# A fused attention and feed-forward kernel: its list of steps in another order, with other buffers and engines for some of them

## The chip, the cores and the metric

One core of one Trainium2 chip runs the whole kernel. The metric is device time in microseconds (us). The core has five engines with queues of their own: TensorE (PE in the profile, with PEld for its weight loads), VectorE (DVE), ScalarE (ACT), GpSimd (POOL), and SyncE (SP), which issues the DMAs. PSUM takes the matmuls' results, SBUF holds the tiles.

## The reference

For 4 batches, 4 heads, 1088 positions and a head dimension of 32, an attention without softmax: queries and keys are sketched with two 8 x 32 matrices, the two sketches are multiplied to 64 features, and the attention is linear in them. Its result, as 4352 tokens of width 128, goes through a multiplicative feed-forward network.

```python
def phi(x):
    a = einsum('rd,bhsd->bhsr', S1, x)
    b = einsum('rd,bhsd->bhsr', S2, x)
    return einsum('bhsi,bhsj->bhsij', a, b).reshape(..., 64)
kv  = einsum('bhsf,bhsd->bhfd', phi(k), v);  z = sum(phi(k), axis=2)
num = einsum('bhsf,bhfd->bhsd', phi(q), kv)
den = einsum('bhsf,bhf->bhs', phi(q), z)[..., None] + 1e-06
x   = (num / den).transpose(0, 2, 1, 3).reshape(4352, 128)
out = (((x @ w1) * (x @ w2)) @ w3) @ w_out        # w1, w2: 128x1024, w3: 1024x1024, w_out: 1024x128
```

## The kernel before

The work is cut into 1181 named steps, each a small function that issues a few instructions. A name has a part ahead of the dot and an action behind it. `ORDER`, a string with all names, is walked once; each step issues its instructions, and every instruction is chained behind the one before it on its engine, so `ORDER` is the order of each engine's queue:

```python
for name in ORDER.split():
    n = len(traced)
    steps.pop(name)()
    ...
for ins, ahead in zip(bulk[UNDER_WAY:], bulk):          # UNDER_WAY = 4
    tc.add_manual_dep(ins, ahead.name, landed, reason="under way")
```

The second loop lets a bulk load go out only when the fourth bulk load ahead of it has landed. Tiles come from pools with a fixed number of buffers ("b" 8, "l" 13, "m" 32, "s" 8, "x" 3, "raw" 3, "q_m" 2); the strings in `SLOTS` say which buffer each tile takes, in the order of allocation, and a tile waits until the readers of that buffer's last tile are done. `POOL` lists the steps on GpSimd instead of VectorE, `CPV` the copies from PSUM on VectorE instead of ScalarE. `WARM` gives idle matmuls that only keep TensorE running, one step `warm{i}` for each entry. The strings were printed by a planner that isn't in the kernel.

The parts, as they follow each other in the main:

- `k0` to `k3`, `kr0`, `kr1`: a batch's keys and values. `lead`, `rest` (line 651) and `gram` (659) build the keys' Gram sums, `T` and `N` (883 to 912) small products, `G` and `ab` (745) sketches, `kp` (677) their products of 128x1024, `kv` (769) their sum with v, `kq` the form that the queries need.
- `q0` to `q4`, `q6`, `qr`: queries. `A`, `C`, `st`, `sh`, `sl`, `sc` (1365 to 1421) make sketches, `al`, `p01`, `p12`, `p2`, `dn`, `de`, `rc`, `bs`, `na` to `nn` (1426 to 1490) denominators and scaled sketches, `phi` (1509) their products, `pT` (1517) transposes them on VectorE, `x` (1527) is 128 matmuls of 32x32 tiles that give the attention's result, `xT` (1540) copies it out of PSUM. `ns` (1494, 1497) is one multiplication and 16 small copies on GpSimd.
- `w1` to `w10`: blocks of weights; `load`, then `c` (263), `m` (484), `j` (495), `a` (501), which turn the float64 words into float32. `f0` to `f7` multiply w3 and w_out into one matrix w3o: `t` (528) transposes a block, `m` (534) multiplies, `o` (538) copies it out. `v.`, `o.S` and the `s` steps of h4 and h6 form sums of blocks.
- `g0` to `g3`: the feed-forward network on 512 tokens each. For each eighth of the hidden width, `a` (1799) and `b` (1809) are two full matmuls each, `c` (1804) copies a to SBUF, `m` (1815) multiplies it by b on VectorE, `o` (1835) are two matmuls with w3o. `oT` (1842), `oS` (1848) and `st` (1556) send the result out.
- `h4`, `h6`: the same for 1024 tokens each with the products saved by a scheme of seven: products `a`, `b` (1673) of half the rows, two of which share the array; copies `ac` to `bi` (1680, 1685); `m11` to `m22` (1707, 1712) and sums `T1` to `T4` (1727 to 1742); products `P1` to `P7` (1759); sums `k1` to `k9` (1767 to 1785).
- `gr`: the network on the 256 remaining tokens.

Of the kernel before, what the change touches and what calls it, by code (L numbers as in the profile page):

```python
# [53 lines left out]
    g4.oS g5.oS g6.oS g7.oS h4.0T2 h4.0T3 h4.0T4 h4.0m11 h4.0m12 h4.0m22 h4.1T1 h4.1T3 h4.1m11  # L54
    h4.1m12 h4.2m11 h4.2m12 h4.2m22 h4.3T4 h4.s2 h6.0T1 h6.0T2 h6.0T4 h6.0m12 h6.0m22 h6.1T1 h6.1T2
    h6.1m11 h6.1m12 h6.1m22 h6.2T4 h6.2m11 h6.2m12 h6.s1 h6.s2 h6.s4 k0.Nf k0.Nh k0.Nr k0.kp1 k1.Nr
    k1.kp1 k2.Nr k2.kp0 k2.kp1 k2.rest0 k3.Nr k3.kp0 k3.kp1 q0.al q0.p01 q0.phi1 q0.sca q1.al q1.p01
    q1.p12 q1.phi q1.sca q2.bs q2.phi0 q3.al q3.bs q3.p01 q3.p12 q3.p2 q3.phi0 q3.sc q3.sl q4.nn
    q4.p2 q4.phi0 q4.phi1 q4.sc q6.al q6.p12 q6.phi1 q6.sc q6.sl qr.p01 qr.p12 s.KS s.Pp s.blk
    s.blkh s.low s.rest  # L60
# [25 lines left out]
w0.load k1.lead0 q0.xc0 q0.xc1 k0.kq w1.a1 k2.max q0.xt1 k1.ab q0.xT0 q0.xT1 g0.4a q1.load g0.5a q1.sm q1.Ct q1.st  # L86
q1.sh k1.rest0 w0.m1 g0.4b g0.6a q1.sl q1.scy q1.sca g0.7a q1.p01 q1.al k1.abt k1.gram0 k1.gram1 k1.gram2 k1.gram3
k1.gram4 q1.p2 w0.c1 w0.c0 g0.4c w0.j1 q3.tr g0.7b g0.5b kr1.abc q3.max q1.p12 k1.Gm q1.dn k1.Gt k1.Ga k1.Gb q1.de
w9.load kh2.load q1.rc q1.bs w0.j0 g0.4m w0.a1 k1.Gc g0.5c g0.7c g0.7m k1.T0 k1.T1 g0.2a v1.zero q1.phi q3.l2 s.AR
# [5 lines left out]
q3.sh k2.T0 k1.kv2 k1.kv3 k1.kv1 k2.T1 k1.kvr k1.kvc kr1.kp g1.2c k2.Ta q2.p12 q2.dn q2.de k2.Tb g0.0m q2.rc g0.6m
q3.sl q3.sc q3.p01 w9.j g1.7m q1.restT q2.bs g1.6a g1.6c w2.c v2.zero q2.phi0 g1.2b k3.loadr g1.3a g1.3c g1.0a g1.5b
g1.3b k1.kqt warm12 w6.c w6.m g0.3b k1.kq g1.5c g1.4a k3.max g1.4c w5.load g1.1b v2.loadr kh3.load k0.Nr q2.load g1.3m
g1.5m g1.2m g1.0c q2.pT0 warm13 g1.0b k2.Tc q2.x g0.3m w9.a1 w5.m q2.xT0 k3.kT0 k2.N0 k2.N1 w5.c q3.al q3.p2 q3.p12
q3.dn w6.j g1.0m q3.de w7.load w2.m g1.4b w7.m w7.c w3.load w10.load w4.load v2.load w2.j k2.Na g1.4m k2.Nb q3.rc
k3.kT1 k3.lead0 q2.restT q3.bs g0.2b g2.6a g2.3a g2.1a g2.5a g2.4a g2.2a w5.j g1.1m g0.2m q3.phi0 k2.Nr g2.2b g2.0a  # L100
g2.3c g2.2c g2.4b g2.5c w3.c g1.6b k3.rest0 w9.a0 g2.4c w2.a0 g2.1c w2.a1 q4.tr k3.gram0 w6.a0 w5.a1 f6.t g2.2m
k3.gram1 k3.gram2 k3.gram3 k3.gram4 q3.pT0 f6.m g2.6b g2.6c g2.0c k3.Gm v.t g2.1b k3.Gt k3.Ga k3.Gb w7.j g2.4m q4.max
g2.7a g2.3b g1.6m q4.l2 w3.m k3.Gc w7.a0 g2.0b f6.o g2.3m w5.a0 w6.a1 v3.zero g2.1m q3.x q4.l1 k3.T0 k3.T1 g2.6m w3.j
g2.7c q4.rm g2.5b g2.5m q3.xT0 q3.load g2.7b g3.0a v3.load w8.load v3.loadr k3.Ta w4.m g3.0c g3.0b g3.0m g3.3a g3.1b
g3.1a g3.3c k3.Tb w3.a0 g3.1c g2.0m k2.kp1 q6.tr k3.Tc g2.7m w7.a1 f4.t g3.6a q3.restT g3.6c q4.A0 w3.a1 q6.max k3.ab
k3.N0 k3.abt k2.kp0 q4.C0 q4.C1 k3.N1 f4.m k3.kp1 g3.6b f0.t f3.t f4.o k3.kp0 f0.m q4.At q6.l2 g3.6m k2.kv0 k2.kv3
g3.1m w4.c w4.j k3.kv0 k3.kv1 k3.kv3 k3.kv2 k3.kvr q4.Ct q4.sm q6.l1 qr.max k3.kvc k2.kv1 k2.kv2 k2.kvr k2.kvc f3.m
w8.c f0.o f3.o w4.a1 w4.a0 g3.7a g3.7c g3.4b g2.0o k3.Na q4.st f1.t qr.l2 q6.rm q4.sh w10.m qr.l1 q4.sl q4.sc g3.5a
g3.4a g3.3b f1.m f1.o w10.c g3.4c g3.4m qr.rm k3.Nb q4.p01 w8.m q4.al k3.Nr k3.kqt g2.4o q6.A0 q6.C0 f2.t g3.3m q4.p2
v.3 q6.C1 k3.kq q6.At w8.j w8.a1 q6.Ct g2.6o g3.0o g3.4o qr.A0 qr.C0 qr.C1 qr.Ct q6.sm w10.j q6.st q6.sh q4.p12 w8.a0  # L110
g3.5b q6.sl w10.a1 q6.sc q4.dn qr.At g3.5c q4.de f5.t q4.rc g1.0o g1.1o q4.na q4.bs q4.nb f2.m q4.nm q4.nr qr.sm q6.al
q6.p01 q6.p2 g0.0o g0.1o q6.p12 f2.o g0.2o g0.6o k2.kqt g0.3o q4.ne g3.5m q4.nn q6.dn k2.kq f5.m f5.o g3.7b g3.2b
g1.6o g0.5o g0.4o w10.a0 qr.st f7.t f7.m g3.2a q4.phi0 q4.phi1 qr.sh qr.sl qr.sc f7.o q4.pT0 g3.2c q4.pT1 g2.5o g0.7o
# [1 line left out]
q6.nn v.1 q4.xT1 q6.phi0 q6.phi1 g1.4o o.S3 q4.xT3 g1.2o q6.pT0 g3.5o g3.7m q6.pT1 g1.3o q6.x qr.p2 q6.xT2 qr.p12
qr.dn qr.de g3.1o g1.7o g3.6o g2.1o qr.rc qr.bs q6.xT3 g1.5o q6.xT0 h4.s1 h4.s3 q6.xT1 q6.ns g3.7o g3.2o qr.phi0
qr.pT0 g1.oT qr.x h4.0b5 h4.0a1 qr.xT0 h4.1a1 g2.oT g2.st h4.0b2 g3.oT h4.0a5 h4.0b1 h4.0bd h4.1b1 h4.0ac h4.s2 h4.s4
h4.1ac v.2 h4.0a6 h4.0bc h4.0bh h4.0ae o.S1 h6.s1 h4.0a2 h4.0ah h4.0b3 h4.1b2 o.S2 o.S4 h4.0ad h4.1a6 h6.s2 h4.0a7
h4.0m11 h4.0b6 h4.1a5 g3.st h4.1bc h4.1b6 h4.1ae h4.1bh v.4 h4.0ag h4.0be h4.0bf h4.1b5 h4.0a3 h4.0af h4.0b7 h4.1a7
h4.1be h4.1b7 h4.1ad h4.0a4 h4.0m12 h4.1a2 h4.0bg h4.1bd h4.1b3 h4.1a3 h4.0m22 h4.0b4 h4.1ag h4.2b1 h4.0ai h4.2a1  # L120
h4.1bf h4.2bc h4.2b2 h4.1ah h4.1a4 h4.2a2 h4.2ac h4.1bg h4.1af h4.1m12 h4.1m22 h4.1b4 h4.3b1 h4.2a6 h4.1ai h4.0m21
g1.st h4.2b5 h4.2ae h4.3a1 h4.2bh h4.1m11 h4.2ah h4.1m21 h4.3bc h4.1T1 h4.2m11 h4.3ac h4.2b6 h4.2be h4.2bd h4.0T1
h4.2a5 h4.2ad h4.3a2 h4.3b2 h4.3bh h4.3b6 h4.2a7 h4.2b7 h4.0T3 h4.3a6 h4.3ae h4.2ag h4.2b3 h4.3ah h4.3be h4.2a3 h4.3a5
h4.3ad h4.3b5 h4.3bd h4.2bg h4.2a4 h4.3b7 h4.3a7 h4.1T3 h4.2af h6.1b1 h4.2bf h4.3m11 h4.3a3 h4.2m22 h4.3bg h4.2b4
h4.2ai h4.3ag h4.2m12 h4.3b3 h6.0a1 h4.2m21 h6.0ac h4.3af h4.3a4 h4.1T2 h6.1bc h4.3b4 h6.1a1 h6.0b1 h6.0a6 h4.3ai
h4.3m21 h6.1b6 h4.3bf h4.2T1 h6.1ac h4.0P7 h4.2P1 h4.1P7 h4.0T2 h4.0P1 h4.0T4 h4.1P2 h4.3T1 h4.3m22 h4.1P5 h4.0P4
h6.0bc h4.2P2 h4.0P2 h4.3P5 h4.3m12 h4.2P5 h4.1P6 h4.2T2 h4.2P6 h4.0P5 h4.2T3 h4.1P1 h4.3T3 h4.3P7 h4.2P7 h4.3P1
h4.3T2 h4.3T4 h4.3P6 h4.2T4 h4.2P4 h6.0ae h4.0P6 h4.3P4 h4.1T4 h6.s3 h4.1P4 h4.k1 h4.k3 h4.3P2 h4.k2 h4.0P3 h4.3P3
h4.2P3 h4.k4 h4.k7 h4.1P3 h6.1be h4.k5 gr.1a h6.0b6 gr.1c h6.0be h6.0a7 h6.0b5 h6.0a5 h6.1a6 h6.0ad h6.1b7 h4.k8 h6.s4
# [1805 lines left out]
```

## Time and profile before

| | |
|---|---|
| median of 3 runs | 248.95 us (248.9 to 249.46) |
| the profiled execution | 248.89 us, its span 246.9 us |
| mean granted clock of TensorE | 1.00 |
| busy: PE, DVE, POOL, ACT | 238.4, 212.2, 154.4, 121.8 us |
| instructions | 6753 |
| DMA | 22.06 MB, mean 89 GB/s |

A group's row gives busy time and mean nanoseconds of one, and behind the second bar the engine's idle time ahead of them with what ended it. A row of the timeline gives start and length in us, engine, line, operation and tiles, and in brackets idle time. A row of the chain gives start, length, engine, tile and line. A row of the waits gives who waits for whom, idle time, count and the longest.

### The profile page before, as it was taken

The page shows a single profiled execution, that of the slowest core. Times are in us where ns is not written, and L with a number is a line of the kernel's source. Part 1 is how long each engine was busy: PE and PEld are TensorE (multiplying, and loading weights), DVE is VectorE, ACT ScalarE, POOL GpSimd, SP SyncE. Part 2 cuts the span into 40 slices and gives each one's busy share as a digit, 9 for nine tenths or more (in the row PEclk, how much of TensorE's full clock was granted, in tenths as well). Part 3 has the DMA queues.
Part 4 walks back from the last instruction along what each step waited for, and adds up shares of the span by engine and source line. Part 5 has one row for each costly group of instructions (what it writes and reads, how often), then busy time and mean ns, then how long its engine had stood idle before and what let it go on. Part 6 is the DMA issues. An engine that isn't in the chain of part 4 may idle for free.

```text
span 246.9 us, 6753 instructions
## 1 busy us (share of the span) xinstructions
PE 238.4 (97%) x2726; PEld 133.7 (54%) x2726; DVE 212.2 (86%) x426; ACT 121.8 (49%) x246; POOL 154.4 (63%) x198
## 2 busy tenths in 40 slices
...
GB/s 202 267 167 324 173 204 185 92 229 135 244 177 230 183 230 142 3 4 0 3 0 0 3 1 3 54 73 4 0 0 0 3 11 74 1 0 3 0 53 96
DMA packets 31934, 22.06 MB, mean 89 GB/s; under 512 B 21280, under 2 KB 26528, under 8 KB 31904
## 3 DMA queue, kind: packets, MB, share of 16 engines
...
q8 instruction: 21, 0.34, 0.6%
q14 instruction: 9, 0.07, 0.1%
...
## 4 chain that ended last, share of the span: by engine, by line
PE 80%; DVE 15%; issue 2%; POOL 1%; ACT 0%; DVEq 0%
PE ps_X L1673 11%; PE ps_o L1759 10%; PE a_ps L1799 9%; PE b_ps L1809 9%; PE ps_o L1835 9%; PE ps_w3o L534 6%; PE ps_Y L1673 6%; PE idle_ps L255 4%; PE ps_Z L1673 3%; DVE ab L1815 3%; PE ps_g L659 2%; PE ps_ac L1374 2%; PE ps_kv L769 2%; PE ps_or L1824 2%; DVE pT L1517 1%
## 5 line engine op out<-in xcount | busy, mean ns | idle before, releaser
L1809 PE MATMUL b_ps<-xT,w 128*128 128x512 f32 (+1 forms) x80 | 36.4, 560 | 0.3 <-DVE ab L1815 0.2
L1673 PE MATMUL ps_X<-xd,wv 64*128 64x512 f32 x112 | 35.6, 595 | 0.0
L1799 PE MATMUL a_ps<-xT,w 128*128 128x512 f32 (+1 forms) x80 | 35.4, 558 | 0.0
L1804 ACT COPY ffa<-a_ps 128x512 f32<-128x512 f32 (+1 forms) x34 | 17.6, 536 | 30.4 <-PE a_ps L1799 30.3
L1680 ACT COPY hc<-ps_X 128x512 f32<-128x512 f32 x37 | 20.7, 589 | 21.2 <-PE ps_X L1673 12.9
L1835 PE MATMUL ps_o<-ab,w3o 128*128 128x512 f32 x64 | 29.4, 597 | 0.0
L1815 DVE TENSOR_TENSOR ab<-ffa,b_ps 128x512 f32<-128x512 f32 (+1 forms) x40 | 23.9, 619 | 3.2 <-PE b_ps L1809 2.5
L501 POOL TENSOR_TENSOR w3c<-w3c,cv_m 128x512 int32<-128x512 int32 x16 | 21.0, 1328 | 6.3 <-DVE w3c L495 6.3
L1799 PEld LDWEIGHTS a_ps<-xT,w 128*128 128x128 f32 x80 | 14.4, 190 | 14.6 <-issue 8.5
L1707 POOL TENSOR_TENSOR hc<-hc 128x512 f32<-128x512 f32 x15 | 19.7, 1327 | 2.9 <-DVE hc L1685 2.9
L1673 PEld LDWEIGHTS ps_X<-xd,wv 64*128 64x128 f32 x112 | 15.2, 186 | 10.4 <-issue 8.3
L1809 PEld LDWEIGHTS b_ps<-xT,w 128*128 128x128 f32 x80 | 14.0, 190 | 12.2 <-issue 7.7
L1673 PE MATMUL ps_Y<-xd,wv 64*128 64x512 f32 x48 | 19.2, 599 | 0.0
L1835 PEld LDWEIGHTS ps_o<-ab,w3o 128*128 128x128 f32 x64 | 11.7, 190 | 13.7 <-issue 13.2
L534 PEld LDWEIGHTS ps_w3o<-wo,w3T 128*128 128x128 f32 x128 | 15.3, 192 | 3.2 <-issue 2.5
L534 PE MATMUL ps_w3o<-wo,w3T 128*128 128x128 f32 x128 | 15.9, 277 | 0.6 <-DVE w3T L528 0.6
L1540 ACT COPY xd<-ps_x 64x256 f32<-64x256 f32 x32 | 11.7, 367 | 7.6 <-PE ps_x L1527 7.2
L538 ACT COPY w3o<-ps_w3o 128x128 f32<-128x128 f32 x8 | 2.0, 270 | 26.3 <-PE ps_w3o L534 26.3
L1759 PE MATMUL ps_o<-hc,w3o 128*64 128x512 f32 x32 | 14.7, 596 | 0.0
L1848 POOL TENSOR_TENSOR oT<-oT,nz 128x512 f32<-128x512 f32 x4 | 4.2, 1049 | 15.6 <-DVE oT L1842 14.4
L263 ACT ACTIVATE cv_c<-raw 128x1024 f32<-128x1024 f32 (+1 forms) x13 | 13.0, 1010 | 1.5 <-DMA raw<-in_moe_w_dram 1.5
L1509 POOL TENSOR_TENSOR ph<-s_al,s_bs 128x1024 f32<-128x1024 f32 x5 | 10.4, 2096 | 4.6 <-issue 4.5
...
## 6 DMA issues: line engine op xcount, KB each, us to landing
raw<-in_moe_w_dram SPq DMA_DIRECT2D x32, 256.0 KB, 5.0
...
raw<-in_moe_w_out_dram SPq DMA_DIRECT2D x4, 256.0 KB, 4.3
```

What stands on the lines that cost most here:

```text
L263: act.activation(dst, hi.bitcast(F32), ACT.Prelu, scale=2.0 ** -112, alpha=-2.0 ** 32)
L501: pool.tensor_tensor(d, d, x["m"][:, i * 512:(i + 1) * 512], ALU.add)
L534: pe.matmul(t["o"], w3T[ko][:, c], wo[:, c], start=c == 0, stop=c == NC - 1)
L1673: pe.matmul(x[bank], stat(j, u)[:, i * 128:(i + 1) * 128], rows(j, u), start=new, stop=True, tile_position=(u * 64, 0), skip_group_check=True)
L1680: cp(n(y))(x[k], x[bank])
L1707: on(f"h{g}.{i}m{k}").tensor_mul(both[0][k], both[0][k], both[1][k])
L1759: pe.matmul(acc_o[bank][half[0]:half[1]], w(i), x(i), start=n == 1, stop=n == (2 if j == 3 else 4), tile_position=(0, half[0]), skip_group ...
L1799: pe.matmul(x["a"][:, :w], w_of(0, c), xT[g][:, c0:c0 + w], start=True, stop=True)
L1804: cp(f"g{g}.{c}{su}c")(x["s"][:, :w], x["a"][:, :w])
L1809: pe.matmul(x["b"][:, :w], w_of(1, c), xT[g][:, c0:c0 + w], start=True, stop=True)
L1815: dve.tensor_mul(ab_sb[g, c][:, c0:c0 + w], x["s"][:, :w], x["b"][:, :w])
L1835: pe.matmul(o_ps[g], w3o[:, c], ab_sb[g, c], start=n == 1, stop=n == NC)
```

## The change

Only `SLOTS`, `WARM`, `POOL`, `CPV` and `ORDER` are edited. The arithmetic of the steps stays.

- `ORDER` is the same for 182 steps, up to `q0.xT1 g0.4a q1.load`, and different behind, with `gr.oT0`, `gr.oT1`, `gr.st1` last in both.
- `WARM` loses its last two entries, and `warm12` and `warm13` with them: 1179 steps.
- `POOL`: 21 steps go from GpSimd to VectorE, 26 from VectorE to GpSimd. `CPV`: 11 copies go from VectorE to ScalarE, 11 from ScalarE to VectorE.
- `SLOTS` is renumbered for the new order.
- The bulk loads behind `w0.load` and those of the second batch go out in another order.

The diff's core (passages of `ORDER` with the same content set against each other):

```diff
 SLOTS = {
...
-    "raw": "012012021020121",
+    "raw": "012012012010110",
...
-WARM = [27, 2, 3, 4, 4, 4, 1, 2, 1, 1, 2, 2, 1, 1]
+WARM = [27, 2, 3, 4, 4, 4, 1, 2, 1, 1, 2, 2]
...
 CPV = set("""
-    g0.1c g0.3c g2.1c g2.5c g2.6c g3.4c h4.0ad h4.0ae h4.0bd h4.1ac h4.2ad h4.k1 h6.2bd h6.3ae
-    k0.kT1 k1.kvc k2.kT1 k2.kq k3.kT0 k3.kT1 k3.kq q0.xc0 q0.xc1
+    g0.3c g0.6c g2.7c g3.0c g3.4c h4.1ad h4.1bc h4.1be h4.2ad h4.3bc h6.2ae h6.3ad k0.kT1 k1.kvc
+    k2.kT1 k2.kq k3.kT0 k3.kT1 k3.kq q0.xc0 q0.xc1 q6.xT0 q6.xT1
...
-k1.Ta k1.Tb s.RC k2.kT1 w0.a0 q1.pt0 k1.N0 q2.tr k1.Tc k1.N1 g0.6c q2.max k1.Na g0.0c w6.load
-w2.load g0.6b g0.1a q1.pt1 k2.lead0 k2.rest0 q1.pc0 q1.pc1 q2.l2 q2.l1 q3.l1 g0.1b q1.x g0.5m q1.xT g0.3c g0.1c g0.1m
-w9.m k1.Nr k2.gram0 ... k2.kT0 q3.rm q2.A0 q2.rm k1.kp0 q2.ab ...
+k1.Ta q1.pt0 k1.Tc g0.6c w0.a0 g0.6b k2.lead0 g0.5b s.RC g0.4c k2.rest0 q1.pc0 q1.pt1 q3.tr g0.5m g0.7m k1.Tb g0.1a
+k2.kT0 k1.kp1 w2.load g0.1b q1.pc1 k1.N0 k1.N1 k3.zero q1.x q2.l1 w9.load k1.Na g0.1c k1.Nr g0.4m k2.gram0 k1.Nb
+k2.gram1 q1.xT g0.3c g0.1m k2.gram2 q3.max q3.l2 q2.rm w9.c k2.gram3 ... k1.kp0 q2.A0 ...
...
-... g1.5b g1.3b k1.kqt warm12 w6.c w6.m g0.3b k1.kq g1.5c g1.4a k3.max g1.4c w5.load g1.1b ...
-g1.5m g1.2m g1.0c q2.pT0 warm13 g1.0b k2.Tc q2.x ...
+... q2.de q3.sh g1.3b w6.c q2.rc ... g0.3b g1.3a k3.kT1 g1.0b g0.3m w5.load g1.3c q3.al k1.kqt ...
+k1.kq q3.p01 k3.max g1.3m g1.4a q3.p2 q2.pT0 w9.a1 q2.x ...
...
-... g3.2a q4.phi0 q4.phi1 qr.sh qr.sl qr.sc f7.o q4.pT0 g3.2c q4.pT1 g2.5o g0.7o
-g0.oT g3.2m g3.3o g2.3o q4.x q4.xT2 q6.de qr.p01 q6.rc q4.xT0 q6.bs q6.nb q6.na g2.2o g2.7o qr.al q6.nm q6.nr q6.ne
-q6.nn v.1 q4.xT1 q6.phi0 q6.phi1 g1.4o o.S3 q4.xT3 g1.2o q6.pT0 g3.5o g3.7m q6.pT1 g1.3o q6.x qr.p2 ...
-... h4.s1 h4.s3 q6.xT1 q6.ns g3.7o g3.2o qr.phi0 qr.pT0 g1.oT qr.x h4.0b5 ...
+... q4.nn q6.na g1.1o g3.2c g3.2m f7.o g2.5o q4.phi0 q4.phi1 g3.5m q4.pT0
+q4.pT1 o.S3 qr.sh q4.x qr.sl g0.7o q6.rc q6.bs q4.xT0 q6.nb qr.sc qr.al q6.nm g2.2o q6.nr q6.ne qr.p01 qr.p2 g1.7o
+q6.nn q4.xT1 g1.5o q6.phi0 g3.5o qr.p12 g0.1o q6.phi1 q6.pT0 g0.0o v.1 qr.dn qr.de qr.rc qr.bs g2.3o qr.phi0 q4.xT2
+q4.xT3 q6.pT1 q6.x q6.xT2 h4.s1 q6.xT0 g3.7o h4.s2 v.2 g0.4o h4.s4 g1.0o q6.xT1 g2.7o qr.pT0 q6.xT3 qr.x qr.xT0 h6.s1
...
+... h4.1m11 q6.ns h4.1m21 h4.3b2 ... h4.1T1 h4.3m11 ... h4.2m12 ... h4.1T4 ... h4.1P7 h4.3P1 h4.1P4 ...
...
-... h6.3P3 gr.2m g5.oT gr.3o1 gr.7o0 ... gr.6o1 gr.0o1 g7.st gr.4o1 gr.oT1 gr.st1
+... h6.2P4 gr.4a gr.7o0 h6.k1 gr.2m gr.2o1 gr.3o0 gr.6b ... h6.1P3 ... h6.2P3 ... gr.5o1 gr.0o0 gr.oT0 gr.oT1 gr.st1
```

In `POOL`, of the steps that the text names: `q1.bs`, `q2.al`, `q2.sc`, `q2.sl`, `k1.kp0`, `h4.1T4`, `h4.3m11`, `qr.al`, `qr.bs` and `qr.phi0` go to GpSimd, `k1.kp1`, `q6.sc`, `q6.sl`, `h4.0T2` and `h4.2m11` to VectorE; `q6.phi0` stays on VectorE and `q6.phi1` on GpSimd.

144 lines of the change are left out of this document (71 added, 73 removed).

## The prediction

> **What bounds the kernel now.** I read the share of each engine first, then the chain of waits, then windows cut where the stages of the kernel change, then the single idle gaps of TensorE.
>
> ```profile
> span 246.9 us, 6753 instructions
> PE 238.4 (97%) x2726; PEld 133.7 (54%) x2726; DVE 212.2 (86%) x426; ACT 121.8 (49%) x246; POOL 154.4 (63%) x198
> PE 80%; DVE 15%; issue 2%; POOL 1%; ACT 0%; DVEq 0%
> ```
> TensorE is busy for 97% of the span and carries 80% of the chain. VectorE, at 86%, is next: where TensorE waits it is mostly for VectorE. So the kernel is a TensorE queue with small holes, and an order can only open or close holes.
>
> ```profile
> core 0: us, PE busy (x) PEld busy (x) DVE busy (x) ACT busy (x) POOL busy (x), PEclk, DMA share, GB/s
> 26.50:115.00 88.50, 86.76 (x1432) 49.19 (x1437) 80.44 (x174) 57.48 (x101) 55.34 (x53) 1.00 0.60 152
> 115.00:150.00 35.00, 33.52 (x319) 17.89 (x302) 31.95 (x61) 8.14 (x22) 22.24 (x20) 1.00 0.00 1
> 150.00:158.00 8.00, 8.00 (x122) 3.77 (x95) 5.51 (x11) 5.90 (x17) 7.17 (x21) 1.00 0.05 9
> 158.00:197.00 39.00, 39.00 (x180) 19.72 (x180) 33.80 (x54) 16.37 (x33) 32.29 (x34) 1.00 0.11 20
> 197.00:247.00 50.00, 46.20 (x222) 23.14 (x220) 42.12 (x71) 14.67 (x30) 21.91 (x23) 1.00 0.17 29
> ```
> The granted clock is 1.00 throughout. The order is the same in both kernels up to about 26.5 us. Behind that TensorE is idle 1.74 us up to 115, 1.48 us up to 150, not at all up to 197, and 3.8 us at the end, which is the tail behind the last matmul. The tail's last steps (gr.oT0, gr.oT1 and gr.st1, listed last in both orders) stay as they are, so I count it unchanged. All the new order can win without doing less TensorE work is therefore 1.74 + 1.48 = 3.2 us, and with the two idle matmuls that it drops 3.8.
>
> **What goes.** The holes behind 26.5 us, one by one, and one of the idle matmuls:
>
> ```profile
> 38.62 0.24 PE L912 MATMUL ps_N<-T_p,P2a 32*32 32x8 f32 x8 [0.22 <-DVE T_p L204]
> 44.10 0.34 PE L659 MATMUL ps_g<-kk 128*32 128x64 f32 x8 [0.60 <-POOL kk L651]
> 61.11 0.27 PE L255 MATMUL idle_ps<-zeros 128*128 128x256 bf16 x1
> 73.86 1.12 PE L1809 MATMUL b_ps<-xT,w 128*128 128x512 f32 x2 [0.23 <-DVE ab L1815]
> PE ps_w3o L534 <- DVE w3T L528: 0.6, 1, 0.6
> 148.41 0.76 PE L1527 MATMUL ps_x<-pT,kq 32*32 32x256 f32 x16 [1.09 <-DVE ab L1815]
> 149.56 1.36 PE L1527 MATMUL ps_x<-pT,kq 32*32 32x256 f32 x48 [0.39 <-DVE pT L1517]
> ```
> The first is k1.N0; the new order has two more g steps ahead of it, each two matmuls of 0.43 us. The second is k2.gram0 behind k2.rest0 on POOL; 22 steps now lie between the two in the listing, where 14 did. The third stands for warm12 and warm13, 2 x 0.27 = 0.54. The fourth, g2.2b, and the fifth, f6.m, get other neighbours. The last two are q6.x. Removed: 0.22 + 0.60 + 0.54 + 0.23 + 0.60 + 1.48 = 3.7 us.
>
> **What comes, 1: more changes of tile shape on TensorE.**
>
> ```profile
> 117.35 1.02 PE L1835 MATMUL ps_o<-ab,w3o 128*128 128x512 f32 x2
> 118.30 0.22 PE L1365 MATMUL ps_ac<-q,AR 64*32 64x64 bf16 x8
> 119.24 1.12 PE L1809 MATMUL b_ps<-xT,w 128*128 128x512 f32 x2
> 131.89 2.58 PE ps_o L1835 x6
> ```
> The last row gives the cadence, 2.58 / 6 = 0.43 us a matmul. The two o matmuls are through after 117.35 + 0.86 = 118.21, the ps_ac group starts at 118.30, 0.09 later; and behind the small group two full matmuls take 1.12 where two in a row take 1.02: about 0.1 us each way. Counted in the two listings, behind the common beginning, the old order changes between full tiles and small ones 47 times, the new one 50 times: 3 x 0.1 = +0.3.
>
> **2: the middle, up to 115 us.** VectorE's load there (80.4 of 88.5 us) is the same in sum: the instructions that go from VectorE to POOL and back nearly balance. But new places are tight: q2.C1 right behind q2.rm, k3.T1 right behind k3.Gb, f6.m still close behind g0.2m. Nothing in the trace prices them, so I bound them: 0, if the plan hits everywhere, and 2.5, the old idle time of this window (1.74) and 0.8 more for a listing that reality had no part in. I take 1.0, under the old 1.74, since three of the old holes have visibly been planned for: +1.0.
>
> **3: q6.x (L1527), where the hole of before was.** The new order has 8 o steps (L1835) of 0.86 us between q4.x and q6.x, the old one 6; with q4.x itself (1.25) and q6.x's first 16 matmuls, that need only q6.pT0 (0.37), TensorE has 8 x 0.86 + 1.25 + 0.37 = 8.5 us of work, while VectorE, from q4.pT1 to q6.pT1, now carries 17 instructions:
>
> ```profile
> 133.57 1.93 DVE L1417 TENSOR_TENSOR s_hl<-ay_A,s_hl 128x128 f32<-128x128 f32 x1
> L1417 DVE TENSOR_TENSOR s_hl<-ay_A,s_hl 128x256 f32<-128x256 f32 x1 | 0.4, 425 | 0.0
> 140.07 0.17 DVE L1450 SCALAR_TENSOR_TENSOR s_rc<-s_d 128x32 f32<-128x32 f32 x1
> 140.67 0.42 DVE L1459 TENSOR_TENSOR s_bs<-ay_C,s_rc 128x256 f32<-128x256 f32 x1
> 142.85 0.42 DVE L1490 TENSOR_TENSOR s_bs<-s_bs,nz 128x256 f32<-128x256 f32 x1
> 143.40 1.95 POOL L1509 TENSOR_TENSOR ph<-s_al,s_bs 128x1024 f32<-128x1024 f32 x1 [4.47 <-issue]
> 145.31 1.71 POOL L1613 TENSOR_TENSOR ws<-w3o 128x256 f32<-128x256 f32 x1
> 143.57 2.86 DVE L1509 TENSOR_TENSOR ph<-s_al,s_bs 128x1024 f32<-128x1024 f32 x1 [0.30 <-DVE s_bs L1490]
> L677 DVE TENSOR_TENSOR kp<-kabt 128x1024 f32<-128x1024 f32 x1 | 1.2, 1219 | 0.0
> L1517 DVE STREAM_TRANSPOSE pT<-ph 128x1024 f32<-128x1024 f32 x6 | 7.3, 1229 | 0.1
> ```
> qr.sl 1.93 (as in before, beside POOL) or 0.42; q6.phi0 2.86 or, by the same shape in kp, 1.22; q6.pT0 and pT1 2 x 1.23; and 13 small ones: in before 11 such steps fill the stretch from 140.07 to 142.85 + 0.42, 3.2 us, so 13 take about 3.8, and with the gaps around them 4.1. That is 11.4 us at the slow lengths and 8.2 at the quick ones, so the wait is 2.9 or 0; with phi0 alone slow 9.9 - 8.5 = 1.4. phi0 is again on VectorE beside q6.phi1 on POOL, so its slow length is what the trace shows for this very pair. qr.sl now stands right behind o.S3, POOL's 1.71 us of ws, and may or may not meet it. I take the middle of 1.4 and 2.9, a little down: +2.0. So this hole does not close; it keeps its size.
>
> The slow phi is 0.17 us behind the start of POOL's phi of 1.95, and 143.40 + 1.95 + 1.22 = 146.57 is where it ends (146.43): it stood still until POOL was done. [...]
>
> **4: qr.x.** Its VectorE work behind q6.x is q6.xT0 and xT1, which the change puts on VectorE, and qr.pT0.
>
> ```profile
> L1540 ACT COPY xd<-ps_x 64x256 f32<-64x256 f32 x32 | 11.7, 367 | 7.6 <-PE ps_x L1527 7.2
> ```
> Four copies each, 8 x 0.37 = 2.9 (ScalarE's length; VectorE's for this shape isn't in the trace), and 0.71 for the transpose (half of 1.23, and overhead): 3.7, against 4 o steps, 3.44. +0.3, between 0 and 1.
>
> **5: h4, from 158 us.** In before TensorE has no hole there. The new order takes q6.ns (a POOL multiplication of 0.20 and 16 copies of 32x8) from ahead of h4 into the middle of its POOL queue: h4.1m11, q6.ns, h4.1T1, 3m11, 2m12, 1T4, and then the third of the P block's products, h4.1P4, wants 1T4. Queued behind q6.ns are those four, and k1 to k9 and VectorE's later sums wait on P. To TensorE the listing gives 24 steps of 0.43 between h4.1m11 and 1P4: 10.3 us.
>
> ```profile
> 150.24 4.79 POOL L1497 COPY nz<-nz 32x8 f32<-32x8 f32 x16
> L1497 POOL COPY nz<-nz 32x8 f32<-32x8 f32 x32 | 7.1, 222 | 1.4
> L1707 POOL TENSOR_TENSOR hc<-hc 128x512 f32<-128x512 f32 x15 | 19.7, 1327 | 2.9 <-DVE hc L1685 2.9
> ```
> POOL needs 5 x 1.33 + 0.20 and the copies: 16 x 0.222 = 3.6, together 10.4; or 4.79, together 11.6. The wait is 0.1 to 1.3; I take +0.6 and keep 0 to 2.3 (below, third rival).
>
> **Sum.** 0.3 + 1.0 + 2.0 + 0.3 + 0.6 = 4.2 come, 3.7 go: +0.5 us. The profiled execution took 248.89 (246.9 of span and 2.0 around it), 0.06 under the median 248.95; so the forecast is **249.4**. That is no change that can be told from none: 0.3%, about what a measurement of this kernel can tell, is 0.75 us. With all bounds low it is 248.9 + 0.3 - 3.7 = 245.5; with all high 248.9 - 3.7 + 0.3 + 2.5 + 2.9 + 1.0 + 2.3 = 254.2.
>
> **Loads, engines, and TensorE's program.** Off TensorE's path I cost the rest at nothing, under these covers. In the new order w5.load takes raw slot 2 from w6, so it waits for w6.c (59.00 + 1.16 in before), where it went out ahead of that copy, and every load behind it in SyncE's queue slips.
>
> ```profile
> 59.00 1.16 ACT L263 ACTIVATE cv_c<-raw 128x1024 f32<-128x1024 f32 x1
> 75.75 1.17 ACT L263 ACTIVATE cv_c<-raw 128x1024 f32<-128x1024 f32 x1 [1.50 <-DMA raw<-in_moe_w_dram]
> raw<-in_moe_w_dram SPq DMA_DIRECT2D x32, 256.0 KB, 5.0
> q8 instruction: 21, 0.34, 0.6%
> ```
> A piece lands in 5 us, so up to 5 us of slip come with it. The cover is ScalarE's idle third (57.48 of 88.5 us are busy). w3.c, at 75.75, waited 1.50 us for its load already; behind it in ScalarE's queue stand the c copies that g2 needs (fourth rival). TensorE's program comes in 21 fetches of q8; next to none of them does before show a hole of TensorE, so planning for them removes nothing.
>
> **The rivals.** *First, faster:* the plan's holes close as listed. qr.sl and phi0 run at 0.42 and 1.22, q6.x waits 0 instead of 1.48, the middle costs 0.5, q6.ns is covered: 0.3 + 0.5 + 0.3 + 0.1 - 3.7 = -2.5, **246.4**. For it: k1.N0, gram0 and q6.x all get more TensorE work ahead of them. Against: the row of 2.86.
> *Second, slower, VectorE in the middle:* VectorE is full there, and each TensorE step with an ab product ahead of it (L1815) waits as g2.2b does; if it falls behind, q3.x, q4.A0 and f4.m wait in one lump. Against the forecast: the middle at 2.5 instead of 1.0 and q6.x at 2.9 instead of 2.0, +2.4, **251.8**. For it: 80.44 of 88.5 us leave VectorE 8.1 us for all its waits on others, and 31.95 of 35 in the next window 3.1. It decides once VectorE's steps behind k2.Tb come more than 1 us later than TensorE asks for them.
> *Third, slower, POOL in h4:* the first six copies of before took 2.17 us, 0.36 each. At that, q6.ns takes 5.8 + 0.2, POOL needs 12.6 and h4.1P4 waits 2.3: 1.7 over my sum, **251.1**. It decides from (10.3 - 6.8) / 16 = 0.22 us a copy, which is the mean of the 32; so it is close.
> *Fourth, slower, loads:* w3.c blocks ScalarE for a further 1.5 us, and g2's products stop for that long: **250.9**.
> *Fifth:* the fetches do slow TensorE by steps too small to be seen as holes, and the plan removes them: at the 0.09 us that a change of shape costs, 21 x 0.09 = 1.9, **247.5**.
>
> **How the numbers follow.** Forecast 0.38, first rival 0.27, second 0.13, third 0.10, fourth 0.07, fifth 0.05. The forecast's own range is 248.4 to 250.4 (q6.x 1.4 to 2.9, the middle 0.5 to 1.5); of its 0.38 some 0.24 lie within 0.75 us of 248.95, 0.02 below, 0.12 above. Faster by over 0.3%: 0.27 + 0.05 + 0.02 = 0.34; within: 0.24; slower: 0.12 + 0.13 + 0.10 + 0.07 = 0.42. The range takes the first rival down to 246.0 (the middle at 0.1) and the slower ones up to 252.0 (third rival with q6.x at 2.9): 246.0 to 252.0; about one in ten lies beyond either end.
>
> **What would show it.** Right: TensorE's idle time up to the counterpart of 115 us about 1 us; one hole of about 2 us ahead of q6.x with releaser pT; q6.phi0 on VectorE over 2.5 us; h4.1P4 with a hole of 0.5 us or so behind POOL hc; the tail 3.8. Wrong: no hole at q6.x (then phi0 or qr.sl ran quick, and it is faster), or a hole above 1 us at any step that I have not named, or TensorE's busy time 1 us away from the old 238.4.

## The result and the profile after

The changed kernel takes 253.08 us (median of 6, 252.12 to 254.04); the kernel before took 249.08 in its 6 runs beside and ahead of them. The ratio is 1.0153 (95% interval 1.0113 to 1.0192): slower, where no change that can be told was forecast. The profiled execution took 253.93 us, its span is 252.1, 5.2 more than before.

The lines of the profile's page that answer to those of before, and the windows, cut where the new kernel breaks:

```profile
span 252.1 us, 6772 instructions
PE 239.4 (95%) x2724; PEld 132.1 (52%) x2724; DVE 211.1 (84%) x427; ACT 120.7 (48%) x240; POOL 159.8 (63%) x203
PEclk9999999999999589999999999999999999999999
PE 78%; DVE 11%; DMA 6%; ACT 2%; issue 2%; POOL 0%; SPq 0%; DVEq 0%; ACTq 0%; POOLq 0%
core 0: us, PE busy (x) PEld busy (x) DVE busy (x) ACT busy (x) POOL busy (x), PEclk, DMA share, GB/s
26.50:80.00 53.50, 51.07 (x909) 26.55 (x904) 47.62 (x113) 37.62 (x67) 31.86 (x38) 1.00 0.75 182
80.00:84.00 4.00, 0.31 (x2) 0.23 (x2) 4.00 (x4) 1.69 (x2) 2.98 (x3) 0.87 0.94 234
84.00:89.00 5.00, 5.00 (x6) 1.96 (x7) 3.08 (x7) 0.59 (x1) 0.00 (x0) 0.50 0.46 141
115.00:150.00 35.00, 35.00 (x329) 19.82 (x328) 31.71 (x69) 11.81 (x26) 23.60 (x21) 1.00 0.01 2
```

Two stretches stand out. From 80 to 84 us TensorE is busy for 0.31 us, while VectorE counts as busy for all 4 (3.02 of them are one instruction, k0.Nr below, which has begun and stands still). From 84 to 89 TensorE is "busy" throughout, but with 6 matmuls, at a granted clock of 0.50. At q6.x, where before had its longest hole, there is none (no idle time stands in brackets):

```profile
152.42 1.50 PE L1528 MATMUL ps_x<-pT,kq 32*32 32x256 f32 x64
```

The chain of waits through that place (start, length, engine, tile, line; lines are one higher than in before):

```profile
78.04 1.25 DVE pT L1518
79.29 3.73 DVE AR L955
83.02 0.10 DVE G_g L218
83.12 0.60 DVE ab L1816
83.77 2.08 PE b_ps L1810 x2
85.84 1.71 PE a_ps L1800 x2
87.55 1.71 PE b_ps L1810 x2
```

L955 is the step k0.Nr: one multiplication of 128x16 numbers, one of the 21 steps that the change moved from GpSimd to VectorE. Behind it in VectorE's queue stand k3.Gm, g2.4m and g2.2m; g2.4m gives back the PSUM bank that g2.1b needs. The two engines' timelines there:

```profile
78.04 1.25 DVE L1518 STREAM_TRANSPOSE pT<-ph 128x1024 f32<-128x1024 f32 x1
79.21 3.81 DVE L955 TENSOR_TENSOR AR<-RC,mask2n 128x16 bf16<-128x16 f32 x1
79.11 0.19 POOL L578 MEMSET v<- 64x128 f32 x1
79.28 1.26 POOL L502 TENSOR_TENSOR wo<-wo,cv_m 128x512 int32<-128x512 int32 x1
80.50 2.48 POOL L502 TENSOR_TENSOR w3c<-w3c,cv_m 128x512 int32<-128x512 int32 x2
```

GpSimd's three additions end at 82.98, k0.Nr at 83.02. On GpSimd the same instruction takes 0.21 us (e1 below), on VectorE at another place 0.13 (e3).

Sized by rows: TensorE waits 3.69 us for VectorE, and then the 6 matmuls from 83.77 to the start of f6.m at 89.05 take 5.28 us where 6 x 0.43 = 2.58 would do: 2.7 for the lower clock. Together 6.4 us, more than the whole difference of 5.2. This execution, at a mean granted clock of 0.986, is one of two such among the six; the other four had 0.993, about half as much time at the lower clock, and three of them took 252.1 to 252.5 us. The other holes that are new, as TensorE's waits:

```profile
PE b_ps L1810 <- DVE ab L1816: 3.7, 1, 3.7
PE ps_g L660 <- issue: 1.4, 2, 0.9
PE ps_kv L770 <- DMA v<-in_v_dram: 0.8, 1, 0.8
PE ps_x L1528 <- DVE pT L1518: 0.7, 1, 0.7
PE b_ps L1810 <- ACT ffa L1805: 0.7, 1, 0.7
```

These are g2.1b, k2.gram3 (0.9 of the 1.4: a stop inside the step, with no engine to wait for), k1.kv0 (v1.load is listed later), qr.x, and g0.7b. Against them stand the 3.7 us that went, as listed in the prediction: none of those steps waits any more, and the two idle matmuls are gone.

### The profile page after: what moved, and what is told of

Its sections match the earlier page's. It is cut to its first block, busy times and chain, and to the rows that moved or that the text cites. A ratio compares the mean times of both kernels' runs of the same rounds, so it can differ in the third digit from the quotient of the medians.

```text
span 252.1 us, 6772 instructions
## 1 busy us (share of the span) xinstructions
PE 239.4 (95%) x2724; PEld 132.1 (52%) x2724; DVE 211.1 (84%) x427; ACT 120.7 (48%) x240; POOL 159.8 (63%) x203
## 4 chain that ended last, share of the span: by engine, by line
PE 78%; DVE 11%; DMA 6%; ACT 2%; issue 2%; POOL 0%; SPq 0%; DVEq 0%; ACTq 0%; POOLq 0%
PE b_ps L1810 10%; PE ps_o L1836 10%; PE ps_o L1760 10%; PE ps_X L1674 9%; PE a_ps L1800 9%; PE ps_w3o L535 6%; PE ps_Y L1674 6%; PE ps_Z L1674 3%; DMA v<-in_v_dram 2%; PE ps_x L1528 2%; DMA k<-in_k_dram 2%; PE ps_g L660 2%; PE ps_kv L770 2%; DMA kh<-in_k_dram 2%; DVE AR L955 1%
## 5 line engine op out<-in xcount | busy, mean ns | idle before, releaser
L1810 PE MATMUL b_ps<-xT,w 128*128 128x512 f32 (+1 forms) x80 | 37.6, 583 | 4.4 <-DVE ab L1816 3.7
L1674 PE MATMUL ps_X<-xd,wv 64*128 64x512 f32 x112 | 39.2, 594 | 0.0
L1800 PE MATMUL a_ps<-xT,w 128*128 128x512 f32 (+1 forms) x80 | 37.1, 574 | 0.0
L502 POOL TENSOR_TENSOR w3c<-w3c,cv_m 128x512 int32<-128x512 int32 x16 | 22.3, 1407 | 13.0 <-DVE w3c L496 11.7
L1708 POOL TENSOR_TENSOR hc<-hc 128x512 f32<-128x512 f32 x16 | 20.6, 1306 | 10.6 <-DVE hc L1686 10.5
L1674 PE MATMUL ps_Y<-xd,wv 64*128 64x512 f32 x48 | 20.4, 591 | 0.0
L1760 PE MATMUL ps_o<-tt,ws 128*64 128x512 f32 x32 | 13.1, 595 | 0.0
L1686 DVE TENSOR_TENSOR hc<-hc,ps_Z 128x512 f32<-128x512 f32 x16 | 10.7, 683 | 2.8 <-ACT hc L1681 1.6
L1681 ACT COPY hc<-ps_Y 128x512 f32<-128x512 f32 x13 | 7.7, 590 | 10.7 <-PE ps_Y L1674 5.3
L1510 POOL TENSOR_TENSOR ph<-s_al,s_bs 128x1024 f32<-128x1024 f32 (+1 forms) x6 | 11.8, 1982 | 0.2
```

Of the source, the lines that this page charges most:

```text
L502: pool.tensor_tensor(d, d, x["m"][:, i * 512:(i + 1) * 512], ALU.add)
L1674: pe.matmul(x[bank], stat(j, u)[:, i * 128:(i + 1) * 128], rows(j, u), start=new, stop=True, tile_position=(u * 64, 0), skip_group_check=True)
L1681: cp(n(y))(x[k], x[bank])
L1708: on(f"h{g}.{i}m{k}").tensor_mul(both[0][k], both[0][k], both[1][k])
L1760: pe.matmul(acc_o[bank][half[0]:half[1]], w(i), x(i), start=n == 1, stop=n == (2 if j == 3 else 4), tile_position=(0, half[0]), skip_group ...
L1800: pe.matmul(x["a"][:, :w], w_of(0, c), xT[g][:, c0:c0 + w], start=True, stop=True)
```

## The experiments

The main theory: k0.Nr stood still on VectorE beside GpSimd, TensorE starved, and its idle time cost the clock. The rivals: late loads or a crowded VectorE, of which the hole is only a symptom; or a step that is slow on VectorE anywhere.

| run | edit | median us | ratio to before, 95% interval |
|---|---|---|---|
| e1_nr_pool | k0.Nr back on GpSimd | 246.80 | 0.9885 (0.9859 to 0.9911) |
| e3_nr_moved | k0.Nr on VectorE, earlier | 247.36 | 0.9915 (0.9892 to 0.9938) |
| e4_short_run | two additions listed later | 252.29 | 1.0114 (1.0084 to 1.0143) |
| e2b_idle_fill | hole filled with idle matmuls | 251.10 | 1.0059 (1.0036 to 1.0082) |
| e4b_two_left | two additions moved ahead | 248.62 | 0.9969 (0.9950 to 0.9989) |
| e7_zero_last | only the memset moved | 247.98 | 0.9940 (0.9918 to 0.9961) |
| e10_swapped | k0.Nr behind k3.Gm | 251.53 | 1.0103 (1.0064 to 1.0141) |
| e5_two_g_steps | e1 and two g steps in k2.gram | 247.61 | 0.9920 (0.9895 to 0.9945) |
| e6_all | e5 and two waits | 246.98 | 0.9910 (0.9882 to 0.9938) |
| e8_two_waits | e1 and two waits | 247.05 | 0.9899 (0.9858 to 0.9941) |
| e9_one_g_step | e8 and one g step in k2.gram | 246.52 | 0.9902 (0.9871 to 0.9934) |

The before of the ratios ran beside each group of runs, with medians of 249.37 (e1, e3, e4), 249.44 (e2b, e4b, e5, e6), 249.53 (e7, e8, e9) and 248.82 us (e10). So it is the ratios that are compared. Where an edit changes the order in which tiles are allocated (e2b, e5, e6, e7, e9), `SLOTS` is renumbered with it.

**One step back.** e1_nr_pool:

```diff
 POOL = set("""
+    k0.Nr
```


> The changed kernel with one step, k0.Nr, back on GpSimd. Theory A (k0.Nr on VectorE stood still for 3.8 us until GpSimd's run of three instructions was over, TensorE starved for 3.7 us at g2.1b and was then granted half the clock for some 5 us): no hole at g2.1b, granted clock 1.00, about 3.9 + 2.7 = 6.6 us less than the 253.1 of the changed kernel: 246 to 247.5. Rival B (late loads, or a VectorE that is too full in the middle, of which the hole is only the place where it shows): a hole of 2 us or more somewhere between 75 and 100 us, 250 or more.

246.80 us, 1.15% under before. The windows of its trace (columns as above, behind the page's row of busy time) have no hole at that place, the clock is 1.00, and k0.Nr is one short row on GpSimd:

```profile
PE 236.9 (97%) x2724; PEld 130.9 (53%) x2724; DVE 207.5 (85%) x426; ACT 120.8 (49%) x240; POOL 160.0 (65%) x204
78.00:84.00 6.00, 6.00 (x25) 3.33 (x25) 6.00 (x13) 4.19 (x6) 5.04 (x6) 1.00 0.94 248
84.00:115.00 31.00, 31.00 (x498) 19.83 (x509) 26.76 (x47) 18.51 (x33) 24.17 (x16) 1.00 0.40 99
80.36 0.21 POOL L955 TENSOR_TENSOR AR<-RC,mask2n 128x16 bf16<-128x16 f32 x1
```
The span, 245.4, is 6.7 under that of the changed kernel, against 6.4 by the rows. So one of the 47 steps that went between VectorE and GpSimd carries the whole loss and more; the rest of the plan is faster than before. The rival of late loads falls: nothing took the hole's place.

Little of that comes from TensorE waiting less. In the two profiled executions it is idle for 246.9 - 238.4 = 8.5 us in before and 245.4 - 236.9 = 8.5 us here (0.5 less behind the common beginning, 0.6 more within it): most of what went came back at other places. What fell is its busy time, by 1.5 us (e3's is 237.0, e7's 236.7). The two idle matmuls account for 0.54 of that; what the remaining 1 us is, no run shows.

**The engine or the place?** e3_nr_moved:

```diff
-... q4.tr k3.rest0 ... g2.3b k0.Nr k3.Gm ...
+... q4.tr k0.Nr k3.rest0 ... g2.3b k3.Gm ...
```


> The changed kernel with k0.Nr still on VectorE, but earlier in its queue, behind q4.tr, where GpSimd is idle. Theory A: k0.Nr takes about 0.2 us there, the time is that of the first run within 0.5 us (246 to 247.5). If the step is slow on VectorE wherever it stands, it stays at 253 and the hole moves ahead by 5 us.

247.36 us; its interval overlaps that of the run before. VectorE's timeline:

```profile
73.70 0.13 DVE L955 TENSOR_TENSOR AR<-RC,mask2n 128x16 bf16<-128x16 f32 x1
```
0.13 us where GpSimd is idle, against 3.81. The step isn't slow on VectorE; the place was.

**What VectorE waited for.** e4_short_run:

```diff
-... w5.a0 ... w6.a1 ... k3.Ta k3.Tb ...
+... k3.Ta w5.a0 w6.a1 k3.Tb ...
```


> The changed kernel with two of GpSimd's three instructions behind k0.Nr (w5.a0 and w6.a1) put later, behind k3.Ta; k0.Nr stays where it is, on VectorE. Theory A, with VectorE shut out until GpSimd's run ends: k0.Nr takes about 1.3 us instead of 3.8, the hole at g2.1b about 1.3, no or little loss of clock, 247.5 to 249. If VectorE waits for something else than GpSimd's run, k0.Nr stays at 3.8 us and the time at 253.

A miss of mine: nothing else stands in GpSimd's queue there, so the two additions ran at the same time as ever, and k0.Nr took 3.80 us again. It serves as a second trace of the same event. e4b_two_left moved them ahead instead:

```diff
-... w6.a0 ... w5.a1 ... w2.a1 ... v3.zero w2.a0 ... w5.a0 ... w6.a1 ...
+... w6.a0 w6.a1 ... w5.a1 w5.a0 ... w2.a1 ... w2.a0 v3.zero ...
```


> The changed kernel with k0.Nr where it is, on VectorE, but with two of the instructions that stood behind it in GpSimd's queue moved ahead (w6.a1 behind w6.a0, w5.a0 behind w5.a1) and v3.zero put last, so that about two instructions (w2.a1, w2.a0) are left of GpSimd's run when k0.Nr comes, where there were three. The first try of this had left the run as it was, since nothing in GpSimd's queue waits there. If VectorE is shut out until the run ends: k0.Nr about 2.4 us, the hole at g2.1b about 2.3, 250 to 251.5. If it is shut out for the one instruction under way: k0.Nr about 1.1, the hole about 1, 247.5 to 249. If k0.Nr is slow for a reason of its own: 3.8 and 252 to 253.

Neither the run's end nor 3.8, but one instruction. The timelines of both engines (in the kernels from here on the same lines have numbers that are 8 lower, in e2b_idle_fill 3 lower):

```profile
78.70 1.21 DVE L947 TENSOR_TENSOR AR<-RC,mask2n 128x16 bf16<-128x16 f32 x1
78.62 2.49 POOL L494 TENSOR_TENSOR wo<-wo,cv_m 128x512 int32<-128x512 int32 x2
```
The first of GpSimd's two additions ends at about 79.88, k0.Nr at 79.91, and the second addition runs on. TensorE still lost 1.5 us at g2.1b (its wait for ab), the clock stayed at 1.00, and the time is 248.62. Wherever else in the traces of before and of the changed kernel VectorE is held up by 0.7 us or more (five rows of before, by 0.9 to 1.7 us; three of the changed kernel, by 0.8 to 1.1), it is for one instruction of GpSimd too, as here in the changed kernel, though the next one follows at once.

```profile
69.19 1.21 DVE L205 SCALAR_TENSOR_TENSOR RC<-N_g,N_t 128x8 f32<-128x8 f32 x1
69.11 1.26 POOL L502 TENSOR_TENSOR w3c<-w3c,cv_m 128x512 int32<-128x512 int32 x1
70.34 1.95 POOL L1510 TENSOR_TENSOR ph<-s_al,s_bs 128x1024 f32<-128x1024 f32 x1
```
So what made it three instructions for k0.Nr in the changed kernel? e7_zero_last and e10_swapped each move one step:

```diff
-... w2.a1 q2.restT v3.zero w2.a0 ... w5.a0 ... w6.a1 ...
+... w2.a1 q2.restT w2.a0 ... w5.a0 ... w6.a1 v3.zero ...
```


> The changed kernel with one edit: v3.zero, GpSimd's small memset just ahead of k0.Nr's time, goes behind w6.a1, so that GpSimd's four additions (w2.a1, w2.a0, w5.a0, w6.a1) follow each other without it, and k0.Nr, on VectorE, comes 0.2 us behind the start of the second of them instead of within 0.1 us of it. If VectorE is shut out until a run of instructions that wait for nothing is over: k0.Nr 3.6 us, the hole as before, 252 to 253. If it is shut out for one instruction, as in the run with two left, and the 3.8 us came from the moment at which it asked: k0.Nr about 1.1, 247.8 to 249.

```diff
-... g2.3b k0.Nr k3.Gm g2.4m ...
+... g2.3b k3.Gm k0.Nr g2.4m ...
```


> The changed kernel with one swap: k3.Gm, 0.2 us long and reading PSUM, goes ahead of k0.Nr in VectorE's queue, so k0.Nr asks 0.1 us later, when GpSimd's memset is over and its next addition is under way. GpSimd's queue is untouched. If the 3.8 us came from the moment at which k0.Nr asked, it takes about 1.1 us now and the time is 247.8 to 249. If they came from the memset and the three additions that stand in GpSimd's queue, it keeps 3.6 and the time 252 to 253.

The two traces, e7_zero_last first:

```profile
78.67 1.22 DVE L947 TENSOR_TENSOR AR<-RC,mask2n 128x16 bf16<-128x16 f32 x1
77.36 2.51 POOL L494 TENSOR_TENSOR wo<-wo,cv_m 128x512 int32<-128x512 int32 x2
79.83 2.50 POOL L494 TENSOR_TENSOR w3c<-w3c,cv_m 128x512 int32<-128x512 int32 x2
```
```profile
77.86 0.15 DVE L210 TENSOR_REDUCE G_g<-ps_g 128x1 f32<-128x32 f32 x1
77.93 3.75 DVE L947 TENSOR_TENSOR AR<-RC,mask2n 128x16 bf16<-128x16 f32 x1
77.76 0.22 POOL L570 MEMSET v<- 64x128 f32 x1
77.92 1.28 POOL L494 TENSOR_TENSOR wo<-wo,cv_m 128x512 int32<-128x512 int32 x1
79.15 2.50 POOL L494 TENSOR_TENSOR w3c<-w3c,cv_m 128x512 int32<-128x512 int32 x2
```
With the memset of 0.2 us out of the way, VectorE gets its turn after one addition, though two more follow without a pause: 247.98 us, 5 us under the changed kernel, for a memset. With the memset in place and k0.Nr later in VectorE's queue it stays shut out for three: 251.53. In the four traces with the memset just ahead (the changed kernel, e4_short_run, e2b_idle_fill, e10_swapped) it is three (3.75 to 3.84 us), in the two without it is one (1.21 and 1.22 us).

e10_swapped doesn't part the memset from the moment of asking, as it was meant to. Against the start of GpSimd's first addition, k0.Nr came only 0.08 us later than in the changed kernel (0.01 behind it instead of 0.07 ahead), and the memset's record (77.76 + 0.22 = 77.98) still wasn't over at 77.93. In e7_zero_last and e4b_two_left it came 0.08 behind the start of an addition. A row of the changed kernel speaks against the moment alone: q6.phi0 asks at 146.83, 0.04 ahead of the start of GpSimd's q6.phi1, while the instruction before that one, here an addition, has 0.07 left:

```profile
146.53 0.37 POOL L1441 TENSOR_TENSOR s_pr<-s_pr 128x64 f32<-128x64 f32 x1 [0.36 <-DVE s_pr L1433]
146.83 1.23 DVE L1510 TENSOR_TENSOR ph<-s_al,s_bs 128x1024 f32<-128x1024 f32 x1
146.87 3.00 POOL L1510 TENSOR_TENSOR ph<-s_al,s_bs 128x1024 f32<-128x1024 f32 x1
```
There VectorE goes first. So the memset is what the four long cases share, and it rests on one run that moves it; why it should have that effect, the traces don't show.

**The clock.** e2b_idle_fill:

```diff
-WARM = [27, 2, 3, 4, 4, 4, 1, 2, 1, 1, 2, 2]
+WARM = [27, 2, 3, 4, 4, 4, 1, 2, 1, 1, 2, 2, 34]
-... g2.2m g2.1b ...
+... g2.2m warm12 g2.1b ...
```


> The changed kernel with 34 idle matmuls (3.6 us) ahead of g2.1b, in a PSUM bank that is free there; k0.Nr stays on VectorE and its stall of 3.8 us stays. If the lower clock comes from TensorE's idle time, the clock stays at 1.00 and the time falls by the 1.8 to 2.7 us that the slow matmuls behind the hole cost: 250.0 to 251.3. If the clock falls for another reason, the time stays at 252 to 253.5 and the granted clock at 0.986 to 0.993.

```profile
79.17 3.87 PE L253 MATMUL idle_ps<-zeros 128*128 128x256 bf16 x34
83.05 1.12 PE L1807 MATMUL b_ps<-xT,w 128*128 128x512 f32 x2
84.01 1.02 PE L1797 MATMUL a_ps<-xT,w 128*128 128x512 f32 x2
```
The stall stays (k0.Nr takes 3.84 us), the matmuls behind it run at 0.43 us again, and the ratio falls from 1.0153 to 1.0059: work that computes nothing wins 2.3 us. The hole of 1.5 us in e4b_two_left cost no clock, that of 3.7 did. How long the lower clock lasts, windows of the changed kernel's trace show, and, in the last two rows, of e10_swapped's:

```profile
82.97:86.36 3.39, 2.59 (x3) 1.18 (x4) 3.20 (x8) 0.00 (x0) 0.01 (x1) 0.50 0.39 94
86.38:89.77 3.39, 3.39 (x8) 1.73 (x7) 1.36 (x4) 0.59 (x1) 0.00 (x0) 0.50 0.61 193
89.79:93.00 3.21, 3.21 (x56) 2.23 (x56) 2.51 (x9) 1.61 (x3) 1.82 (x2) 1.00 0.95 203
82.69:86.09 3.40, 3.40 (x5) 1.35 (x4) 2.87 (x7) 0.24 (x1) 0.00 (x0) 0.50 0.42 132
86.11:89.00 2.89, 2.89 (x27) 2.32 (x25) 1.99 (x4) 0.63 (x3) 0.55 (x1) 1.00 0.60 160
```
In the traces' record of the clock, the stretch at 0.50 lasts 6.83 us in the changed kernel (82.96 to 89.78) and 3.41 in e10_swapped and e4_short_run, half as long; the stretch at 1.00 ahead of it is 78.51 us long in all three, 23 times 3.41. All of these are whole multiples of 3.413 us, and so are the stretch behind the fall in the changed kernel, 163.84 us, 48 times, and the one at 1.00 in before, 242.35 us, 71 times: I read that as a clock that changes on a grid of 3.41 us, an inference from these lengths. The step of the grid just ahead of each fall held 2.9 to 3.1 us of the hole, and 0.3 to 0.5 us of work. In the changed kernel the first step at 0.50 still held 0.8 us of the hole (the first row), and a second step at 0.50 followed; in e10_swapped's first one TensorE was busy throughout (3.40 of 3.40 us), and 1.00 followed. It would also fit that the hole's price changes from run to run with its place on such a grid: one of six in e10_swapped took 249.68 us at a mean clock of 1.00, the other five, at 0.993, 251.52 to 252.47. The hole of that one run is in no trace.

**The stop at k2.gram3.** The sum of small matmuls there (64 or 32 columns each) halts in its middle, waiting for no engine. In the trace's DMA records a fetch of 16 KB on q8 begins at 43.43 and lands at 44.78; the last small matmul begins at 44.92 and the next at 46.02, 1.24 behind the landing. (I take q8's fetches for TensorE's program: in all traces the one that comes at 26 to 29 us starts when 1014 or 1015 of TensorE's matmuls and weight loads have begun, and 20 of the 21 start within 41 of the same count in before and in the changed kernel.) In the traces of the changed kernel, e1, e3, e4, e2b, e4b, e7, e8 and e10 TensorE halts each time with exactly 1702 recorded matmuls and weight loads begun, and goes on 1.2 to 1.5 us behind the landing of that fetch. In before the same fetch landed at 43.34, while TensorE stood at gram0 for k2.rest0, and 1.25 us later it had begun only 1538: the wait for rest0 covered the fetch. That points to the program running out, though no run changed the fetch itself. e5_two_g_steps puts slow work there:

```diff
-... k2.gram2 q3.max ... k2.gram3 k2.gram4 w6.m ... q2.C0 q2.C1 ... g1.5a g1.5c ... g1.1a g1.1c ...
+... k2.gram2 g1.5a g1.1a q3.max ... k2.gram3 k2.gram4 g1.5c g1.1c w6.m ... q2.C0 q2.C1 ...
```


> The first run's kernel (k0.Nr on GpSimd, 246.8 us) with two feed-forward steps, g1.5a and g1.1a (2 x 0.86 us of TensorE, some 8 instructions), put between k2.gram2 and k2.gram3, where TensorE stood still for 1.1 to 1.4 us with no wait on any engine. If TensorE there had used up its program faster than it was fetched (some 230 instructions in 1.5 us), the hole is gone or under 0.3 us: 245.4 to 246.2. If the hole belongs to k2.gram3 itself, it stays: 246.5 to 247.2.

The stop is gone (no wait of TensorE over 0.15 us in k2.gram), but the time isn't: 247.61, above both ranges. The slow work would cover any wait that ends by itself, so this run doesn't tell a fetch from another cause. Without the two steps behind q2.C1 TensorE waits for VectorE there, to empty the banks that q3.A0 needs. The row of its waits:

```profile
PE ps_ac L1358 <- DVE ay_C L1384: 1.2, 1, 1.2
```
So the cover was only taken from one wait to the other. e6_all, e8_two_waits and e9_one_g_step add edits to e5, e1 and e8:

```diff
-(e6) ... w0.m1 w0.m0 ... g0.5c ...            q6.xT1 g2.7o qr.pT0 ...
+(e6) ... g0.5c w0.m1 w0.m0 ...                qr.pT0 q6.xT1 g2.7o ...
-(e8) ... w0.m1 w0.m0 ... g0.5c ... g0.7c ...  q6.xT1 g2.7o qr.pT0 ...
+(e8) ... w0.m1 ... g0.5c ... g0.7c w0.m0 ...  qr.pT0 q6.xT1 g2.7o ...
+(e9) e8, and g1.5a behind k2.gram2, g1.5c behind k2.gram4
```


> The kernel of the run before this one, and also g0.5c ahead of w0.m1 in ScalarE's queue (g0.7b waited 0.9 us for it) and qr.pT0 ahead of q6.xT1 in VectorE's (qr.x waited 0.9). If the holes are each what they look like, they add up: 1.5 to 1.8 us less than the run before, 243.8 to 244.8. If VectorE's or ScalarE's queue only moves the wait elsewhere, no less than 245.4.

> The first run's kernel (k0.Nr on GpSimd, 246.8 us) with w0.m0 behind g0.7c in ScalarE's queue (g0.7b waits for g0.7c, which gives its bank free; moving g0.5c ahead did nothing to it) and qr.pT0 ahead of q6.xT1 in VectorE's. 0.6 us less at g0.7b and 0.3 at qr.x (0.6 of 0.9 were left inside qr.x in the run before): 245.6 to 246.3. If the stop of TensorE's program at k2.gram3 takes up what is won ahead of it, 246.3 to 246.8.

> The run before with one feed-forward step, g1.5a, between k2.gram2 and k2.gram3; g1.1a stays behind q2.C1. With two steps put there the stop had moved from TensorE's 1702nd recorded instruction to its 1928th, at q2.C1. If a stop comes where a block of the program is used up before the next one is there, one step takes 0.9 us off the first stop and leaves 0 to 0.5 at the second: 245.0 to 245.9. If the stops only change places, the time is that of the run before.

e6_all: g0.7b's wait stays (0.6), since it waits for g0.7c and not g0.5c, and qr.x keeps 0.4 of its 0.7: 246.98. e8_two_waits took 247.05, above both ranges: the wait of 0.7 at g0.7b is gone, but 0.2 comes back at g0.2a, and the stop at k2.gram3 grows from 1.2 us idle in e1 to 1.5, so that most of what was won ahead of the stop is lost again by its end. e9_one_g_step took 246.52, outside the range of 245.0 to 245.9: the stop is gone (under 0.1 us idle), and g1.1a waits 0.9 for VectorE's ay_C. Its trace is of one of the longest of its twelve runs, 248.39, with a further wait of 1.0 us for a load at the start. My reading of a second stop "at the 1928th instruction", on which I expected something of e9, was wrong: that was the wait for ay_C. The intervals of e1, e5, e6, e8 and e9 overlap, so none of the later edits is shown to win anything over e1, the simplest of those that beat both kernels.

## Why the prediction was wrong

The range ended at 252.0 and the time was 253.08. The forecast was +0.5 us, no change that can be told; it became +4.0. Three of the signs that I had named against it came: no hole at q6.x, a hole above 1 us at a step that I had not named (g2.1b), and TensorE's busy time 1.0 us away from 238.4.

- **The step that failed** is the second term of the sum, the middle up to 115 us: 1.0 taken, 2.5 as the upper bound. It measured 0.7 (g0.7b) + 0.9 (k2.gram3) + 0.8 (k1.kv0) + 3.7 (g2.1b) = 6.1 of waits, and 2.7 of clock. I bounded it from before's idle time in that window (1.74), which says how well the old plan fitted, not what a new one can hit. The steps that go from GpSimd to VectorE were counted as balancing in sum; each had to be looked at for what runs beside it. The rows were there: the 2.86 of q6.phi0, which I used in one place only.
- **The contention** was the right mechanism at the wrong step. I took it for q6.phi0 and qr.sl (2.0 us); there q6.x doesn't wait at all. The rows of the changed kernel, shown above with the memset, have phi0 0.04 us ahead of GpSimd's phi1: VectorE took 1.23 us, and GpSimd stood still and took 3.00, where it took 1.95 in before. In before phi0 had come 0.17 us behind, and VectorE paid with 2.86. So in both traces the one of this pair that came later waited; I had reckoned as if VectorE lost again. And I had reckoned with a wait for one instruction of GpSimd; k0.Nr's, 3.81 us long, lasted for three in a row.
- **The clock** was not in the sum. All rows of before stood at 1.00, and its longest hole behind the common beginning was 1.1 us, so nothing there priced a hole of 3.7.
- **More changes of tile shape**, the first term, were to add 0.3 to TensorE's work. The size of that term alone can't be read from the runs, but without the lower clock the new order's busy time is 1.5 us smaller (e1), not larger.
- **qr.x** was 0.7 for 0.3 forecast: the eight copies on VectorE took 3.47 us (0.43 each), where I had ScalarE's 0.37. **h4.1P4** didn't wait (0.6 forecast); q6.ns was covered, and the P block's first matmul (h4.1P7) came 0.3 later than the cadence. **The tail** was unchanged.
- **The rivals.** The first (faster, 246.4) has nearly the time that the change gives without k0.Nr's place, 246.80, but partly by luck: it had the holes close and only 0.5 come in the middle, where e1's trace has only 0.5 us less idle time behind the common beginning, and a smaller busy time that the rival didn't name. The second named VectorE in the middle, with 251.8 and a chance of 0.13; it had the place, but as a queue that is crowded, not one instruction that is shut out. The fifth held that planning for the fetches might win time; what the traces show is a stop that the new order uncovered.
- **What went** went as listed (3.7 us), and GpSimd's k2.rest0 no longer holds gram0; but 0.9 came back in the same sum as the stop in k2.gram3, a wait that the old one had covered, as far as the traces point.
